# Linear attention and a cosine feed-forward layer on one core: the key maxima as two float32r parts, the projection loaded by ScalarE, another order table

## The chip, the cores and the metric

The kernel runs on one core of one Trainium2 chip. A core has five engines with queues of their own: TensorE (PE in the profile; its weight loads are shown as PEld), VectorE (DVE), ScalarE (ACT), GpSimd (POOL) and SyncE (SP), which here only starts transfers. Each engine takes its instructions strictly in order, and waits at an instruction until the semaphores that it needs have been raised. The metric is the device time of one execution in microseconds (us). Of the kernel before there are three times, 1094.05, 1092.6 and 1094.47 us, with a median of 1094.05 us.

## The reference

For 8 batches and 8 heads, with 576 positions and 64 channels a head:

```python
def phi(x):
    proj = np.einsum('bhsd,df->bhsf', x, w_phi)                 # 64 -> 128 features
    proj = proj - np.max(np.abs(proj), axis=-1, keepdims=True)
    return np.concatenate([np.exp(proj), np.exp(-proj)], axis=-1)
q_p, k_p = phi(q), phi(k)
kv  = np.einsum('bhsf,bhsd->bhfd', k_p, v);  z = np.sum(k_p, axis=2)
num = np.einsum('bhsf,bhfd->bhsd', q_p, kv)
den = np.einsum('bhsf,bhf->bhs', q_p, z)[..., None] + 1e-06
x   = (num / den)                       # then 4608 tokens x 512 channels
h   = x @ w_in                          # 512 -> 2048
out = (h * np.cos(h)) @ w_out           # 2048 -> 512
```

Each row of a projection has its largest absolute value taken off before the two exponentials. That subtraction, for the keys, is what the change touches.

## The kernel before

**Two stages, interleaved.** The attention is cut into 32 units `u` of two heads each (`attention(u)`, L427). The feed-forward layer is cut into 15 visits `v` of a block of 512 tokens and a list of 128-wide slices of the hidden layer (`visit(v)`, L741). The weights of the layer are split once into two float32r parts, a high and a low one (`convert(ft)`, L353), so that three fast float32r products stand for one float32 product: twelve matmuls of 128x128 by 128x512 per first product (L798), and four times three per second product (L832 to L834). The attention matmuls are plain float32, which TensorE runs as two passes: one matmul in the code is two records in the trace.

**The keys of a unit.** `k_mm` (L493) and its tail (`k_end`, L568) project the keys into three PSUM banks, two of 128x512 and one of 128x128. VectorE takes the row maxima (`k_max`, L580): a 128x4 tile for each of the two large banks, 128x1 for the tail. In units 0 to 7 (`K_SUMS = range(8)`) TensorE then adds the negated maxima to the bank itself (`k_sub`, L590): the weights are `minus`, a 128x128 matrix with -1 on its diagonal, and the moving operand is the tile of maxima, each value repeated 128 times by a broadcast view. ScalarE reads the bank and writes both exponentials (`exp_k`, L598). In units 8 to 31 VectorE subtracts instead (L585). The exponentials go into the sums `kv` and `z` (`kv_mm`, L642 and L648), which ScalarE copies out of PSUM.

**The queries.** `q_mm` (L455) projects them, ScalarE copies the result (L462), VectorE reduces it across partitions (L466, L474, L476), spreads the maxima (L480), GpSimd subtracts (`q_sub`, L484), and ScalarE takes the exponentials (L603). `z_mm` (L681) and `n_mm` (L691) form denominators and numerators, and VectorE divides.

**Order.** All work is built as `Step` objects, each with its engine and a function that issues its instructions. A table of step numbers, `ORDER` (L86), gives one order for all of them, and each engine's queue is that order cut down to its own steps. Nothing is reordered later. `plan()` (L240) goes over the table and gives each PSUM tile one of eight banks: before the change it keeps a clock for each engine, adds up the steps' written costs, and takes the bank that comes free first by that clock. The costs and the names `port` and `table` serve only that choice.

**Start.** SP loads `w_phi` into both halves of `wphi` (L309), then the queries and keys of unit 0 and of unit 1, then the first weights. GpSimd writes `halfpi`, `minus` and the constant columns of the value tiles. On GpSimd's queue lie the subtractions for the queries and the last three steps of the first four weight slices (L387, L54 and L393).

Of the kernel before, what the change touches and what calls it, by code (L numbers as in the profile page):

```python
# [17 lines left out]
P = 128  # L18
# [7 lines left out]
def phi_attention_then_cos_ffn(ctx: ExitStack, tc: tile.TileContext, qT, kT, vS, vT, w_phi, w_in, w_out, out):  # L26
# [41 lines left out]
    class Step:  # L68
# [15 lines left out]
    SWITCH = dict(e=1.3, s=1.3, full=0.21, left=0.145, quarter=0.12, upper=0.2)  # L84
    SHAPE = dict(mm1="full", mm2="full", one="full", k_mm="upper", k_end="full", t_mm="upper", t_end="full", s_mm="full", k_sub="full", kv_mm="left", n_mm="left", z_mm="quarter", q_mm="upper")
    ORDER = [  # L86
# [151 lines left out]
    LATENCY = dict(PE=0.35, ACT=0.25, DVE=0.2, POOL=0.25, SP=2.2)  # L238

    def plan():  # L240
        free = dict.fromkeys(LATENCY, 0.0)
        free["port"] = 0.0
        table = {}
        last = {}
# [702 lines left out]
```

## Time and profile before

| | |
|---|---|
| median of the three times | 1094.05 us |
| time of the profiled execution | 1094.05 us |
| its span in the trace | 1092.3 us |
| outside the span (difference of the two) | 1.75 us |
| TensorE busy | 1075.4 us, 98% of the span |
| VectorE busy | 725.2 us, 66% |
| ScalarE busy | 717.2 us, 66% |
| GpSimd busy | 127.3 us, 12% |
| TensorE clock granted | 1.00 |

"Busy" is the time in which at least one instruction of the engine was running. Matmuls overlap, so the duration of a matmul in the trace is longer than the time that it keeps the next one away: the distance from start to start is the cost in a row of matmuls. A line such as `PE bank L590 <- DVE mk_u__850 L580: 1.3, 1, 1.3` in the view of waits says that TensorE, at line 590, stood idle for 1.3 us in total, once, 1.3 us at longest, until VectorE's line 580 had written `mk`.

### The profile page before, as it was taken

To read this page: it belongs to the slowest core of one execution; us is meant where nothing else is said; L and a number is where in the kernel's file an instruction comes from. 1 tells how busy PE (TensorE), PEld (TensorE's weight loads), DVE (VectorE), ACT (ScalarE), POOL (GpSimd) and SP (SyncE) were. 2 spreads that over 40 slices of the span, in tenths; PEclk is the share of its full clock that TensorE was granted. 3 is DMA by queue.
4 is the path that set the end of the run, shared out by engine and by line. 5 is a ranking of instruction groups with operands and counts; after the bars stand their busy time and mean duration, and the time that the engine had idled before them with its cause. 6 is when DMAs were issued, how large, how long until landed. Compare 5 with 4: busy or idle time off the path is not lost.

```text
span 1092.3 us, 19509 instructions
## 1 busy us (share of the span) xinstructions
PE 1075.4 (98%) x7664; PEld 827.7 (76%) x7664; DVE 725.2 (66%) x1298; ACT 717.2 (66%) x1386; POOL 127.3 (12%) x91
## 2 busy tenths in 40 slices
PE   7999999999999999999999999999999999999998
PEld 4656666778888887788677787787777778888886
DVE  5899999989889868555577366773665354343432
ACT  5888889977666587657567666857667654443533
POOL 2654221000000011101031011110111000000000
PEclk9999999999999999999999999999999999999999
DMA  6564664356667355555241651345211620630441
GB/s 193 150 192 121 193 193 142 97 167 208 224 203 242 109 196 159 195 180 222 55 149 69 205 185 46 106 176 192 93 61 61 250 99 2 222 125 20 146 191 48
DMA packets 92603, 160.71 MB, mean 147 GB/s; under 512 B 43744, under 2 KB 52064, under 8 KB 84320
## 3 DMA queue, kind: packets, MB, share of 16 engines
q1 hardware_dynamic: 92512, 159.48, 43.9%
q8 instruction: 60, 0.98, 0.4%
q14 instruction: 31, 0.25, 0.1%
HBM read 117.51 MB, written 41.94 MB: 146 GB/s over the span
## 4 chain that ended last, share of the span: by engine, by line
PE 86%; DVE 6%; issue 0%; DMA 0%; ACT 0%; DVEq 0%
PE bank L798 35%; PE bank L832 12%; PE bank L833 12%; PE bank L834 12%; PE bank L691 4%; PE bank L642 4%; PE bank L681 2%; PE bank L455 2%; PE bank L493 2%; PE bank L648 1%; PE bank L568 0%; DVE g_c__1102 L809 0%; DMA out<-o_last 0%; DVE m_u__975 L466 0%; DVE g_c__1972 L809 0%
## 5 line engine op out<-in xcount | busy, mean ns | idle before, releaser
L813 ACT ACT_TABLE_LOAD x22 | 28.2, 1283 | 0.4
L484 POOL TENSOR_TENSOR pq_u__3673<-pq_u__3673,bq_u__4170 128x576 f32<-128x576 f32 x2 | 3.6, 1796 | 186.1 <-DVE bq_u__4170 L480 186.1
L872 DVE TENSOR_TENSOR o<-bank,o 128x512 f32<-128x512 f32 x24 | 16.2, 679 | 0.7 <-DMA o<-sums 0.5
L881 DVE COPY o<-bank 128x512 f32<-128x512 f32 x16 | 10.8, 677 | 5.9 <-PE bank L834 4.7
L603 ACT ACT_TABLE_LOAD x11 | 14.1, 1283 | 0.2
L879 ACT ACTIVATE o<-bank 128x512 f32<-128x512 f32 x16 | 9.5, 593 | 5.5 <-PE bank L834 5.5
L598 ACT ACT_TABLE_LOAD x10 | 12.8, 1283 | 0.2
L798 PE MATMUL bank<-xh_c__7472,w 128*128 128x512 f32 x32 | 12.8, 400 | 0.0
L798 PE MATMUL bank<-xh_c__6688,w 128*128 128x512 f32 x32 | 12.8, 399 | 0.0
L798 PE MATMUL bank<-xh_c__5272,w 128*128 128x512 f32 x32 | 12.8, 399 | 0.0
L798 PE MATMUL bank<-xh_c__4458,w 128*128 128x512 f32 x32 | 12.7, 396 | 0.0
L798 PE MATMUL bank<-xh_c__7041,w 128*128 128x512 f32 x32 | 12.5, 390 | 0.0
L798 PE MATMUL bank<-xh_c__5868,w 128*128 128x512 f32 x32 | 12.5, 390 | 0.0
L798 PE MATMUL bank<-xh_c__8219,w 128*128 128x512 f32 x32 | 12.5, 390 | 0.0
L798 PE MATMUL bank<-xh_c__5790,w 128*128 128x512 f32 x32 | 12.5, 390 | 0.0
L798 PE MATMUL bank<-xh_c__7889,w 128*128 128x512 f32 x32 | 12.5, 390 | 0.0
L798 PE MATMUL bank<-xh_c__6645,w 128*128 128x512 f32 x32 | 12.5, 390 | 0.0
L798 PE MATMUL bank<-xh_c__5941,w 128*128 128x512 f32 x32 | 12.5, 390 | 0.0
L798 PE MATMUL bank<-xh_c__4514,w 128*128 128x512 f32 x32 | 12.5, 390 | 0.0
L798 PE MATMUL bank<-xh_c__4696,w 128*128 128x512 f32 x32 | 12.5, 390 | 0.0
L798 PE MATMUL bank<-xh_c__7074,w 128*128 128x512 f32 x32 | 12.5, 390 | 0.0
L798 PE MATMUL bank<-xh_c__8223,w 128*128 128x512 f32 x32 | 12.5, 390 | 0.0
(3837 smaller groups left out, 4061.7 us busy)
## 6 DMA issues: line engine op xcount, KB each, us to landing
w<-w_parts SPq DMA_DIRECT2D x48, 1024.0 KB, 5.0
w_parts<-w SPq DMA_DIRECT2D x16, 1024.0 KB, 5.5
vmain<-vS SPq DMA_DIRECT2D x32, 256.0 KB, 4.7
out<-o SPq DMA_DIRECT2D x32, 256.0 KB, 3.0
sums<-o SPq DMA_DIRECT2D x24, 256.0 KB, 3.3
o<-sums SPq DMA_DIRECT2D x24, 256.0 KB, 3.2
vtail<-vT SPq DMA_DIRECT2D x64, 16.0 KB, 3.7
out<-o_last SPq DMA_DIRECT2D x4, 256.0 KB, 2.0
```

The costliest lines, as they stand in the source:

```text
L455: PE.matmul(out=ps[j], lhsT=wphi[r, :], rhs=d["qr"][r, hf * HALF:(hf + 1) * HALF], start=True, stop=True)
L493: PE.matmul(out=ps[j][:, P * s:P * s + P], lhsT=x[r, P * s:P * s + P], rhs=wphi[r, :], start=(s == 0), stop=w, skip_group_check=True)
L603: ACT.activation(out=e[:, s, :], in_=d["pq"][:, j * S:(j + 1) * S], func=AF.Exp, scale=1.0 - 2.0 * s)
L642: PE.matmul(out=acc[c:c + 64, n, i, :], lhsT=e[:, s, P * n + c:P * n + c + 64], rhs=vmain[u % 2][:, s, i, :], start=(s == 0 and i == 0 and ...
L681: PE.matmul(out=ps[32 * g:32 * g + 32], lhsT=d["z"][:, 2 * n + j, :], rhs=d["eq", j][:, n, hf * HALF:(hf + 1) * HALF], start=(n == 0), sto ...
L691: PE.matmul(out=d["nps", hf][64 * j:64 * j + 64], lhsT=d["kv"][:, 2 * n + j, :], rhs=d["eq", j][:, n, cut[hf]], start=(n == 0 and hf == 0) ...
L798: PE.matmul(out=h, lhsT=a[:, cs], rhs=d[b, kt], start=(k == 0), stop=(k == 3 * KT - 1))
L813: ACT.activation(out=m["g"], in_=m["g"], func=AF.Sin, bias=halfpi, scale=1.0)
L832: PE.matmul(out=a, lhsT=gh[:, t], rhs=w[:, 0], start=first, stop=False)
L833: PE.matmul(out=a, lhsT=gh[:, t], rhs=w[:, 1], start=False, stop=False)
L834: PE.matmul(out=a, lhsT=gl[:, t], rhs=w[:, 0], start=False, stop=last)
L872: DVE.tensor_tensor(out=o, in0=bank(acc[tb]), in1=o, op=ALU.add)
```

## The change

1. **The maxima in two parts.** A new step `k_parts` on GpSimd stands between `k_max` and `k_sub` in units 0 to 7, three to a unit, 24 in all. It writes a float32r copy of the maxima (`hi_of`, one `tensor_scalar`) and the float32r remainder (`lo_of`, one `tensor_tensor`), each 128x4 or 128x1. `k_sub` issues two float32r matmuls in place of one in float32. `minus` becomes float32r, made from `minus_f` by one more GpSimd instruction at the start.
2. **The projection's load** is issued by ScalarE's queue instead of SP's.
3. **Seven extra matmuls** (`WARM = 7`) of a zeroed 128x128 float32 tile by itself go to bank 7 ahead of the planned steps. VectorE zeroes the tile. Their result is not used.
4. **Another order table**, with the 24 new steps. On every engine but GpSimd it holds the same steps as before. Counted in the two tables: matmul steps that differ in tile shape from the one before them on TensorE are 180 before and 173 after, and changes of ScalarE's function table are 44 before and 46 after.
5. **`plan()`** gives a new PSUM tile the bank whose last user stands earliest in the table, and no longer uses costs. The costs written at the steps are changed too, and decide nothing any more.

```diff
-    ORDER = [
-        0, 41, 2, 5, 3, 6, 7, 4, 8, 10, 11, 43, 46, 16, 57, 9, 12, 1192, 18, 20, 13, 44, 45, 48, 61, 19, 17, 58, 21,
...
+        place = {steps[x]: i for i, x in enumerate(ORDER)}
+        owner = [None] * len(banks)
+
+        def last(b):
+            return -1 if b is None else max(place[v] for v in b.users)
...
+                    b.slot = min(range(len(banks)), key=lambda i: last(owner[i]))
...
-        SP.dma_start(out=wphi[64 * j:64 * j + 64, :], in_=w_phi)
+        ACT.dma_start(out=wphi[64 * j:64 * j + 64, :], in_=w_phi)
...
-    minus = const.tile([P, P], F32, name="minus")
-    POOL.memset(minus, -1.0)
-    POOL.affine_select(out=minus, in_=minus, pattern=[[-1, P]], compare_op=ALU.is_equal, fill=0.0, base=0,
+    warm = const.tile([P, P], F32, name="warm")
+    DVE.memset(warm, 0.0)
+
+    minus_f = const.tile([P, P], F32, name="minus_f")
+    POOL.memset(minus_f, -1.0)
+    POOL.affine_select(out=minus_f, in_=minus_f, pattern=[[-1, P]], compare_op=ALU.is_equal, fill=0.0, base=0,
                        channel_multiplier=1)
+    minus = const.tile([P, P], F32R, name="minus")
+    hi_of(POOL, minus, minus_f)
...
+    WARM = 7
...
+        def k_parts(i):
+            tag = "pk" if i < 2 else "pk_t"
+            m = d["mk", i]
+            p = d["mp", i] = new(tag, [P, 2, NSLOT if i < 2 else 1], F32R, f"mp_u{u}_", "mp" + tag)
+            hi_of(POOL, p[:, 0], m)
+            lo_of(POOL, p[:, 1], m, p[:, 0])
+
         def k_sub(i):
...
-            PE.matmul(out=pv, lhsT=minus, rhs=d["mk", i].unsqueeze(2).broadcast_to([P, n, P]), start=False, stop=True,
-                      skip_group_check=True)
+            for r in range(2):
+                PE.matmul(out=pv, lhsT=minus, rhs=d["mp", i][:, r].unsqueeze(2).broadcast_to([P, n, P]), start=False,
+                          stop=(r == 1), skip_group_check=True)
...
             if u in K_SUMS:
-                kms[i] = Step("PE", 0.86 if i < 2 else 0.22, lambda i=i: k_sub(i), [kms[i]], use=[kb[i], pks[i]], kind="a.k_sub")
+                kms[i] = Step("POOL", 0.35, lambda i=i: k_parts(i), [kms[i]], use=[pks[i]], port=True, kind="a.k_parts")
+                kms[i] = Step("PE", 0.46 if i < 2 else 0.14, lambda i=i: k_sub(i), [kms[i]], use=[kb[i], pks[i]], kind="a.k_sub")
...
+        for _ in range(WARM):
+            PE.matmul(out=banks[7][:, 0:P], lhsT=warm, rhs=warm, start=True, stop=True, skip_group_check=True)
         for x in plan():
             x.fn()
```

The heads of the queues that the new table gives, in step names (unit in brackets): TensorE `k_end(0)`, two `q_mm(0)`, `k_sub(0)` of the tail, `q_mm(1)`, `k_mm(0)`, `q_mm(1)`, `k_end(1)`, `k_mm(1)`, three `k_sub`, then `kv_mm(0)`; before, four `q_mm`, `k_mm(0)`, `k_mm(1)`, `k_sub(0)`, two `k_end`, four `k_sub`, then `kv_mm(0)`. ScalarE: four `q_copy(0)`, `exp_k(0)` of the tail, four `q_copy(1)`, the first `w.scale` (L371 and L372), the two large `exp_k(0)`. SP: loads of unit 0 and unit 1, first weights, values of unit 0, as before. GpSimd: three `k_parts(0)` and one `k_parts(1)`, then the first `q_sub(0)`, with the other `k_parts` between subtractions and weight steps from there on.

More of the change, by code (lines that the diff above doesn't have):

```diff
@@ L356, in convert @@
         slot = w_slot[ft] = Buf("w")
-        name, eng, cost = ("POOL", POOL, 2.4) if ft in W_POOL else ("DVE", DVE, 1.22)
+        name, eng, cost = ("POOL", POOL, 2.4) if ft in W_POOL else ("DVE", DVE, 1.135)
         def load():
@@ L609, in attention @@
             d["kb", i] = kb[i]
-        main = Step("PE", 0.88, lambda: k_mm(0), [ld], take=kb[:2] + pks[:2], use=[b["kr"]], kind=phase + "k_mm")
-        tail = Step("PE", 0.22, lambda: k_mm(1), [ld], take=[kb[2], pks[2]], use=[b["kr"]], kind=phase + "k_end")
+        main = Step("PE", 0.89, lambda: k_mm(0), [ld], take=kb[:2] + pks[:2], use=[b["kr"]], kind=phase + "k_mm")
+        tail = Step("PE", 0.14, lambda: k_mm(1), [ld], take=[kb[2], pks[2]], use=[b["kr"]], kind=phase + "k_end")
         for i in range(3):
-            cost = (1.3 if i < 2 else 0.55) if u not in K_SUMS else 0.67 if i < 2 else 0.28
+            cost = (1.32 if i < 2 else 0.51) if u not in K_SUMS else 0.6 if i < 2 else 0.21
             kms.append(Step("DVE", cost, lambda i=i: k_max(i), [tail if i == 2 else main], use=[kb[i], pks[i]],
@@ L621, in attention @@
             e = Buf("ek" if i < 2 else "ek_t")
-            eks.append(Step("ACT", 1.06 if i < 2 else 0.42, lambda i=i: exp_k(i), [kms[i]] + gate, take=[e], use=[pks[i]] + ([kb[i]] if u in K_SUMS else []),
+            eks.append(Step("ACT", 1.045 if i < 2 else 0.4, lambda i=i: exp_k(i), [kms[i]] + gate, take=[e], use=[pks[i]] + ([kb[i]] if u in K_SUMS else []),
                             table="e", kind=phase + "exp_k"))
@@ L667, in attention @@
                         kind=phase + "kv_mm")
-        ko = Step("ACT", 0.6, kv_out, [last], use=[acc, b["kv"]], kind=phase + "kv_out")
+        ko = Step("ACT", 0.45, kv_out, [last], use=[acc, b["kv"]], kind=phase + "kv_out")
         N0 = CT
```

70 lines of the change are left out of this document (20 added, 50 removed), and 300 rows, old and new, of the table ORDER.

## The prediction

> **What bounds the kernel now.** I read the page's first part, then busy time by stretches, then TensorE's waits. The stretches have these columns: from and to, length, then busy time and number of instructions of PE, PEld, DVE, ACT and POOL, the granted clock, the DMA share and GB/s.
>
> ```profile
> PE 1075.4 (98%) x7664; PEld 827.7 (76%) x7664; DVE 725.2 (66%) x1298; ACT 717.2 (66%) x1386; POOL 127.3 (12%) x91
> ```
>
> ```profile
> 0.00:5.00 5.00, 0.00 (x0) 0.00 (x0) 0.00 (x0) 1.28 (x1) 1.42 (x15) 1.00 0.36 102
> 5.00:30.00 25.00, 21.98 (x213) 14.79 (x214) 18.49 (x38) 16.49 (x40) 9.30 (x6) 1.00 0.62 192
> 30.00:100.00 70.00, 67.95 (x798) 43.46 (x797) 65.11 (x122) 59.41 (x130) 39.28 (x21) 1.00 0.48 146
> 100.00:200.00 100.00, 97.66 (x1089) 65.38 (x1089) 94.56 (x201) 87.18 (x193) 24.21 (x17) 1.00 0.56 173
> 200.00:1000.00 800.00, 799.97 (x5181) 631.61 (x5181) 514.03 (x891) 516.63 (x962) 53.13 (x34) 1.00 0.44 147
> 1000.00:1088.00 88.00, 87.86 (x388) 72.44 (x386) 32.32 (x49) 36.21 (x63) 0.00 (x0) 1.00 0.30 108
> 1088.00:1092.30 4.30, 0.00 (x0) 0.00 (x0) 0.69 (x1) 0.00 (x0) 0.00 (x0) 0.89 0.65 245
> ```
>
> TensorE is the bound. From 200 to 1000 us it is idle for 0.03 us, so each microsecond of its work that goes away, and each wait that goes away ahead of 200 us, comes off the end. All its idle time is 16.9 us (1092.3 less 1075.4): 5.27 us before the first matmul, some 4.4 us after the last one, where the last tile is copied and stored, and 7.1 us of waits in between, nearly all of them ahead of 200 us. There VectorE is almost as full: 65.11 of 70 us and 94.56 of 100 us. That is the stage in which the change lies.
>
> ```profile
> PE bank L455 <- DMA qr_u__117<-qT: 5.3, 1, 5.3
> PE bank L590 <- DVE mk_u__293 L580: 1.6, 1, 1.6
> PE bank L590 <- DVE mk_u__850 L580: 1.3, 1, 1.3
> PE bank L455 <- DMA qr_u__121<-qT: 1.1, 1, 1.1
> PE bank L798 <- DVE pk_u__1058 L585: 0.8, 1, 0.8
> ```
>
> The first wait is the start. Of the others only two are waits of `k_sub` for its maxima, so 22 of the 24 subtractions now find them ready.
>
> **The subtraction in two parts.** Four neighbours in the timeline give the float32 price by start distances, and one row of the chain gives the float32r price (start, length, engine, line):
>
> ```profile
> 72.57 0.38 PE L590 MATMUL bank<-mk_u__940,minus 128*128 128x128 f32 x2
> 72.79 1.02 PE L590 MATMUL bank<-mk_u__936,minus 128*128 128x512 f32 x2
> 73.65 1.02 PE L590 MATMUL bank<-mk_u__930,minus 128*128 128x512 f32 x2
> 74.60 1.24 PE L455 MATMUL bank<-qr_u__789,wphi 64*128 64x288 f32 x8
> ```
>
> ```profile
> 1038.90 8.16 PE bank L798 x36
> ```
>
> A large float32 `k_sub` keeps TensorE for 73.65 - 72.79 = 0.86 us, a tail for 72.79 - 72.57 = 0.22 us. Float32r with 512 columns costs 8.16/36 = 0.227 us, so two parts cost 0.45 us, and 16 large ones save 16 x 0.41 = 6.5 us. No row shows float32r with 128 columns. Its bounds are a quarter of 0.227 us a part (0.11 us for two) and no gain at all (0.22 us). I take 0.16 us, halfway, so 8 tails save 0.5 us, with 0 to 0.9 us as ends. That the moving operand is a broadcast view is no new cost, since the float32 form has the same view. **Sum: -7.0 us.**
>
> **The order's own work on TensorE.** The tables hold the same steps, with 7 fewer changes of tile shape. The price of one:
>
> ```profile
> 82.06 0.50 PE L798 MATMUL bank<-xh_c__439,w 128*128 128x512 f32 x1
> 82.40 0.40 PE L798 MATMUL bank<-xh_c__660,w 128*128 128x512 f32 x1
> ```
>
> After a change the next matmul starts 82.40 - 82.06 = 0.34 us later, against 0.227 us in a row: 0.11 us each. **-0.8 us**, with 0 and twice that as ends, as the shapes differ.
>
> **The start.** Rows of the timeline, and landing times of the transfers (last column, us from issue):
>
> ```profile
> 0.81 1.21 SPq L309 DMA_DIRECT2D wphi<-w_phi  x2
> 2.07 0.58 SPq L437 DMA_DIRECT2D qr_u__117<-qT  x1
> 2.69 0.43 SPq L438 DMA_DIRECT2D kr_u__118<-kT  x1
> 5.27 2.29 PE L455 MATMUL bank<-qr_u__117,wphi 64*128 64x288 f32 x8 [5.27 <-DMA qr_u__117<-qT]
> 6.60 0.41 ACT L462 ACTIVATE pq_u__130<-bank 128x288 f32<-128x288 f32 x1 [4.51 <-PE bank L455]
> 8.67 2.29 PE L455 MATMUL bank<-qr_u__121,wphi 64*128 64x288 f32 x8 [1.10 <-DMA qr_u__121<-qT]
> 10.75 1.92 PE L493 MATMUL bank<-wphi,kr_u__118 64*128 64x128 f32 x16
> ```
>
> ```profile
> 59.94 1.24 PE L455 MATMUL bank<-qr_u__610,wphi 64*128 64x288 f32 x8
> 67.93 1.06 PE L493 MATMUL bank<-wphi,kr_u__798 64*128 64x128 f32 x16
> ```
>
> ```profile
> kr_u__118<-kT SPq DMA_DIRECT2D x1, 320.0 KB, 3.4
> wphi<-w_phi SPq DMA_DIRECT2D x2, 32.0 KB, 2.1
> ```
>
> With `wphi` on ScalarE's queue SP issues everything 1.26 us earlier (2.07 - 0.81). ScalarE does nothing then but load a table, so two issues of 0.6 us there cost nothing while its first real work starts at 6.6 us. TensorE's first step is now `k_end(0)`, which needs the keys, the second transfer: issued at 1.4 us, landing 3.4 us later, 4.8 us. That is **-0.5 us**. The ends are 0, if `wphi` is what arrives last, and -1.26 us.
>
> Early matmuls run at half pace: `q_mm` of a unit takes 2.29 us twice, and 1.24 us at 60 us; `k_mm(0)` takes 1.92 us against 1.06 us. That is 2 x 1.05 + 0.86 = 3.0 us. The granted clock in the rows reads 1.00 throughout, so it does not show this. The seven extra matmuls fall into idle time ahead of the data: each is two passes of 128 columns at half pace, so about twice the tail's 0.22 us, seven make 3.1 us, from about 1.1 to 4.2 us. A gap of 0.6 us to the data follows. In the rows the pace doubled only after some 3.5 us without a gap (from 8.67 us; the 2.3 us ahead of the gap there were not enough). I take two thirds of the 3.0 us: **-2.0 us**, with 0 and -3.0 us as ends. The Trainium skill, "TensorE: Matmul & The Clock Gate", section "What's actually happening", says that the clock follows a free-running window of about 3.4 us, so the warm-up is a time and not a count of matmuls; the case's trace agrees with that length, and by the rule the seven alone fall short of a full window, so that the gain would be anything between the two ends, run by run.
>
> **Waits that move.** ScalarE's new queue puts the first weight scaling ahead of the two large `exp_k(0)`:
>
> ```profile
> 12.41 1.14 ACT L371 ACTIVATE w_t_f__193<-w_raw_f__166 128x1024 f32<-128x1024 f32 x1 [0.99 <-DMA w_raw_f__166<-w_out]
> 14.75 1.08 ACT L598 ACTIVATE ek_u__198<-bank 128x512 f32<-128x512 f32 x2 [0.20 <-PE bank L590]
> 18.04 1.15 PE L642 MATMUL bank<-vmain,ek_u__198 128*64 128x65 f32 x32
> 24.44 0.49 PE L590 MATMUL bank<-mk_u__293,minus 128*128 128x128 f32 x2 [1.65 <-DVE mk_u__293 L580]
> 25.96 0.27 PE L691 MATMUL bank<-eq_u__268,kv_u__274 128*64 128x64 f32 x1
> ```
>
> The scaling starts when its weights land, at 12.41 - 1.26 = 11.15 us; its two instructions take 2.2 us, the exponentials 1.1 us, and 0.2 us go to the handover: the first `kv_mm` can start at 14.6 us, against 18.04 us. From there to the first `n_mm` TensorE took 7.9 us, 1.65 us of it waiting at a `k_sub(2)` that now stands behind that `n_mm`: with the 0.5 us that two cheaper `k_sub` save on this way, 14.6 + 6.3 - 0.5 = 20.4 us, against 25.96 us, 5.5 us earlier. All six `k_sub` ahead of it account for 1.8 us, start and pace for 2.5 us, and the other 1.2 us are waits saved. I count 0.8 of them, as other steps change places too: **-0.8 us**, with 0 and the 1.65 us of that wait as ends.
>
> Against it stands the detour through GpSimd. No row shows a small arithmetic instruction there. Bounds are
>
> ```profile
> 0.98 0.11 POOL L322 MEMSET vmain<- 128x8 f32 x1
> 1.45 0.29 POOL L315 TENSOR_SCALAR_AFFINE_SELECT minus<-minus 128x128 f32<-128x128 f32 x1
> ```
>
> 0.11 us for a write of 128x8 and 0.29 us for a pass over 128x128: two instructions take 0.22 to 0.58 us, and with one more handover each maximum arrives about 0.6 us later. Behind a waiting `k_sub` stands all of TensorE's queue, and `exp_k` with its `kv_mm` is late next. Where other matmuls stand between `k_max` and `k_sub`, as for 22 of 24 now, they hide it; without that cover it is 24 x 0.6 = 14 us. I take 1.5 us, the two that already wait and a fraction of the rest: **+1.5 us**, ends 0 and, for all of them exposed by half, 7 us. The extra instruction on `minus` and the zeroing of `warm` lie in the first 5 us, ahead of any use. Two more table loads cost ScalarE 2.6 us, in stretches where it has 13 us to spare in 100. The bank choice changes no instruction.
>
> **Sum:** -7.0 - 0.8 - 0.5 - 2.0 - 0.8 + 1.5 = -9.6 us. The profiled execution is its span 1092.3 us and 1.75 us around it, 1094.05 us, which is the median of the three. Forecast: **1084.5 us**.
>
> **Rivals.** *The waits shrink further* (12%). All 7.1 us of waits are there to be removed, and the keys no longer hold TensorE. If the new table removes 4 us more than I count and the detour stays hidden, the time is 1084.5 - 1.5 - 4 = 1079 us. Against it: VectorE has little idle time to give.
>
> *VectorE becomes the bound* (18%). In the stretch from 30 to 200 us VectorE idles for 10.3 us (4.89 + 5.44). Its work does not shrink, so TensorE can come forward only by VectorE's earlier start, 1.3 us, and by what VectorE's idle time can give. With half of that the gain ends at 1.3 + 5.2 = 6.5 us: 1087.5 us. Speaks for it: three of the four waits shown behind the start are for VectorE. Against it: the table can put more second-layer matmuls, which ask less of VectorE, among the units.
>
> *Two parts cost as much as one float32 product* (6%). If a broadcast float32r operand ran at float32's pace the 7.0 us would be missing: 1091.5 us. Line 798's 0.227 us speaks against it.
>
> *GpSimd and VectorE get in each other's way* (9%), the slower side:
>
> ```profile
> L476 DVE TENSOR_TENSOR m_u__287<-m_u__286 x4: 185/186/2285, 21.1 to 23.9; 32x36 f32<-32x36 f32 x4
> 21.00 2.35 POOL L387 TENSOR_TENSOR w_t_f__195<-w_t_f__195,w_t_f__193 128x1024 f32<-128x1024 f32 x1 [2.79 <-ACT eq_u__271 L603]
> ```
>
> A 0.186 us instruction of VectorE took 2.285 us from 21.1 us on, just while GpSimd's 2.35 us multiplication ran. Each `k_parts` is a new reader there. If its 0.4 us stops VectorE each time, that is 24 x 0.4 = 9.6 us on the fuller engine, with VectorE as the bound as above: 1094.05 - 6.5 + 9.6 = 1097 us. It decides from about 6.5 us of added stops, and below that it only eats the gain. Against it: VectorE's maxima are read from PSUM, and its long stops come from the 2.4 us instructions, which stay as they are. The Trainium skill, "SBUF — State Buffer", section "Who interferes with whom", holds that the pair of ports is locked for a whole instruction and the other engine fully blocks; the 2.285 us agree.
>
> **How the numbers follow.** 55% for the forecast; its own range from the bounds is 1080 to 1088 us. The rivals have 12, 18, 6 and 9%. The range of 1079 to 1091.5 us leaves out the slower rival and a little of the fastest. A measurement of this kernel tells about 0.2%, 2.2 us, from no change. Faster by that holds for the forecast, the first two rivals and a part of the third, 0.87; 0.05 stays within it; 0.08 is slower.
>
> **What would show it.** Line `k_sub` as float32r with starts 0.23 us apart; TensorE's busy time lower by 9 to 11 us; matmuls ahead of 5 us, and `q_mm(0)` near 1.3 us; first `kv_mm` near 14.6 us and first `n_mm` near 20.5 us; waits of `k_sub` on GpSimd of 1 to 2 us in total; idle TensorE from 200 us on still near zero. Wrong would be: waits ahead of 200 us above 12 us, VectorE idle there as long as now, many small VectorE instructions of over 0.4 us, or new waits for weights behind 200 us.

## The result, and the profile after

The changed kernel takes 1108.09 us (median of four executions, 1106.01 to 1109.66), the kernel before 1094.07 us beside it: a ratio of 1.0129, with a 95% interval of 1.0110 to 1.0149. It is 14.0 us slower, where 9.6 us faster was forecast, and outside the range. The profiled execution took 1109.66 us, 1107.7 us of them its span.

In the changed kernel all lines after the start have other numbers: `k_end` is L548, `k_max` L560, VectorE's subtraction L565, `k_sub` L578, `k_mm` L473, `q_mm` L435, `z_mm` L670, `n_mm` L680, `invert` L686. The two instructions of `k_parts` are recorded under their helpers, L51 and L54. First the busy line of the page and the busy time by stretches, with the columns explained in the prediction.

```profile
PE 1077.8 (97%) x7678; PEld 835.6 (75%) x7678; DVE 735.2 (66%) x1299; ACT 718.5 (65%) x1388; POOL 140.2 (13%) x140
```

```profile
30.00:70.00 40.00, 39.98 (x550) 26.21 (x549) 37.39 (x75) 37.93 (x92) 29.45 (x41) 1.00 0.58 177
70.00:120.00 50.00, 41.34 (x386) 28.52 (x386) 48.40 (x87) 37.16 (x74) 21.10 (x18) 0.97 0.43 145
120.00:200.00 80.00, 77.38 (x898) 53.27 (x893) 73.05 (x155) 69.19 (x156) 18.11 (x12) 0.98 0.47 144
200.00:400.00 200.00, 200.00 (x1062) 162.45 (x1062) 172.20 (x252) 138.40 (x235) 6.43 (x4) 1.00 0.56 189
400.00:600.00 200.00, 190.55 (x1455) 145.64 (x1454) 122.30 (x228) 124.22 (x246) 19.12 (x12) 0.97 0.41 138
```

TensorE is idle for 1107.7 - 1077.8 = 29.9 us, 13.0 us more than before. Of the 29.9 us, 9.45 us lie between 400 and 600 us, where TensorE had been busy throughout, and 8.66 us between 70 and 120 us, where VectorE is now at 48.40 of 50 us. The busy time did not fall but rose by 2.4 us, although the subtraction became cheaper; 3.36 us of it are the seven extra matmuls. Three stretches show a clock below 1.00. In the first two (1 - 0.97) x 50 + (1 - 0.98) x 80 = 3 us of full pace are missing, as far as two decimals tell; for the third see the narrower rows below. The longest waits of TensorE name the places:

```profile
PE bank L680 <- DVE dn_u__4563 L686: 5.4, 1, 5.4
PE bank L680 <- DVE dn_u__4825 L686: 3.4, 1, 3.4
PE bank L578 <- POOL mp_u__1174 L51: 1.9, 1, 1.9
PE bank L548 <- DVE pk_u__1298 L565: 1.8, 1, 1.8
PE bank L473 <- DVE pk_u__2314 L565: 1.5, 1, 1.5
PE bank L680 <- DVE dn_u__1578 L686: 1.4, 1, 1.4
```

The two largest are `n_mm` behind `invert`, a pair of steps that the prediction never mentions. The timeline at the first of them (start, length, engine, line), the stretches ahead of it and behind it, and the stretch behind the second:

```profile
410.38 0.44 DVE L686 TRANSPOSE_TENSOR_REDUCE dn_u__4563<-bank 128x9 f32<-128x288 f32 x1
410.87 0.37 PE L680 MATMUL bank<-eq_u__4328,kv_u__4422 128*64 128x64 f32 x1 [5.42 <-DVE dn_u__4563 L686]
411.35 1.06 PE L680 MATMUL bank<-eq_u__4328,kv_u__4422 128*64 128x512 f32 x1
```

```profile
405.00:411.00 6.00, 0.58 (x6) 0.13 (x4) 5.86 (x11) 3.80 (x6) 0.00 (x0) 0.80 0.08 31
411.00:420.00 9.00, 9.00 (x99) 5.94 (x100) 2.91 (x8) 2.33 (x8) 0.00 (x0) 0.76 0.10 31
445.00:450.00 5.00, 5.00 (x22) 2.43 (x23) 2.87 (x7) 0.00 (x0) 0.00 (x0) 0.66 0.83 270
```

TensorE stands still for 5.42 us while VectorE works without a break (5.86 of 6 us) through its queue towards a reduction of 0.44 us. Then it runs with the clock at 0.76, and behind the second wait at 0.66: 9 x 0.24 + 5 x 0.34 = 3.9 us of full pace are missing behind the two. The code says why it waits:

```python
d["nps", 0], d["nps", 1] = bank(nps)[:, 0:N0], bank(zps)[:, HALF:HALF + S - N0]   # z_mm
PE.matmul(out=d["nps", hf][64 * j:64 * j + 64], ...)                              # n_mm
DVE.tensor_reduce(out=dn, in_=d["zps"].rearrange("p (j t) -> p j t", t=32), ...)  # invert
```

`n_mm` writes its last 64 columns into the bank in which `invert` reads the denominators. They are other columns, but it is one tile, and so the two steps are ordered by their places in the table. Whichever stands second waits for the other. In the table before, `n_mm` of units 16 and 31 stood ahead of `invert`, and `n_mm` of unit 15 stood 74 places behind it, time enough for VectorE. In the new table `invert` stands ahead in all three units, 1 to 4 places before its `n_mm`. In unit 7 it stood 8 places ahead and now stands 7 ahead, with other work of VectorE before it; that is the wait of 1.4 us. The place alone does not make a wait: in the table before, `invert` stood ahead by 5 to 8 places in units 10, 22 and 27 as well, and that trace has no wait for `dn`. It takes a VectorE that comes late.

### The profile page after: what moved, and what is told of

It is laid out like the page before. It is cut to its first block, busy times and chain, and to the rows that moved or that the text cites. A ratio compares the mean times of both kernels' runs of the same rounds, so it can differ in the third digit from the quotient of the medians.

```text
span 1107.7 us, 19590 instructions
## 1 busy us (share of the span) xinstructions
PE 1077.8 (97%) x7678; PEld 835.6 (75%) x7678; DVE 735.2 (66%) x1299; ACT 718.5 (65%) x1388; POOL 140.2 (13%) x140
## 4 chain that ended last, share of the span: by engine, by line
PE 83%; DVE 6%; ACT 2%; DMA 1%; issue 1%; SPq 0%; DVEq 0%
PE bank L787 33%; PE bank L821 11%; PE bank L822 11%; PE bank L823 11%; PE bank L680 5%; PE bank L631 4%; PE bank L670 2%; PE bank L435 2%; PE bank L473 2%; PE bank L637 1%; PE bank L548 0%; DMA qr_u__1767<-qT 0%; DVE m_u__1213 L456 0%; DMA o<-sums 0%; DVE g_c__1244 L798 0%
## 5 line engine op out<-in xcount | busy, mean ns | idle before, releaser
L787 PE MATMUL bank<-xh_c__6814,w 128*128 128x512 f32 x32 | 13.1, 410 | 0.0
L787 PE MATMUL bank<-xh_c__4554,w 128*128 128x512 f32 x32 | 12.8, 401 | 0.0
L787 PE MATMUL bank<-xh_c__5459,w 128*128 128x512 f32 x32 | 12.8, 400 | 0.0
L787 PE MATMUL bank<-xh_c__8108,w 128*128 128x512 f32 x32 | 12.7, 396 | 0.0
L787 PE MATMUL bank<-xh_c__6987,w 128*128 128x512 f32 x32 | 12.5, 392 | 0.0
L787 PE MATMUL bank<-xh_c__6816,w 128*128 128x512 f32 x32 | 12.5, 392 | 0.0
L787 PE MATMUL bank<-xh_c__4756,w 128*128 128x512 f32 x32 | 12.5, 392 | 0.0
L787 PE MATMUL bank<-xh_c__7212,w 128*128 128x512 f32 x32 | 12.5, 391 | 0.0
L787 PE MATMUL bank<-xh_c__4731,w 128*128 128x512 f32 x32 | 12.5, 391 | 0.0
L787 PE MATMUL bank<-xh_c__4810,w 128*128 128x512 f32 x32 | 12.5, 391 | 0.0
L787 PE MATMUL bank<-xh_c__5372,w 128*128 128x512 f32 x32 | 12.5, 390 | 0.0
L787 PE MATMUL bank<-xh_c__8235,w 128*128 128x512 f32 x32 | 12.5, 390 | 0.0
L787 PE MATMUL bank<-xh_c__6016,w 128*128 128x512 f32 x32 | 12.5, 390 | 0.0
L787 PE MATMUL bank<-xh_c__8243,w 128*128 128x512 f32 x32 | 12.5, 390 | 0.0
L787 PE MATMUL bank<-xh_c__7897,w 128*128 128x512 f32 x32 | 12.5, 390 | 0.0
L787 PE MATMUL bank<-xh_c__5919,w 128*128 128x512 f32 x32 | 12.5, 390 | 0.0
L787 PE MATMUL bank<-xh_c__9384,w 128*128 128x512 f32 x32 | 12.5, 390 | 0.0
```

Source lines behind the costliest of these rows:

```text
L787: PE.matmul(out=h, lhsT=a[:, cs], rhs=d[b, kt], start=(k == 0), stop=(k == 3 * KT - 1))
```

## The experiments

All of them in one table. The kernel before ran beside each group, and runs of different groups are compared by the difference from it.

| kernel | median, us | before beside it, us | difference, us | ratio, 95% interval |
|---|---|---|---|---|
| changed kernel | 1108.09 | 1094.07 | +14.0 | 1.0110 to 1.0149 |
| changed, `invert` behind `n_mm` | 1092.19 | 1094.03 | -1.8 | 0.9974 to 0.9993 |
| changed, old bank choice | 1107.71 | 1093.75 | +14.0 | 1.0109 to 1.0139 |
| before, parts alone | 1102.81 | 1094.03 | +8.8 | 1.0071 to 1.0101 |
| before, parts, four GpSimd steps moved | 1098.59 | 1092.91 | +5.7 | 1.0026 to 1.0056 |
| before, new bank choice alone | 1104.29 | 1093.87 | +10.4 | 1.0077 to 1.0109 |
| changed, old table | 1112.36 | 1094.03 | +18.3 | 1.0154 to 1.0186 |
| changed, no parts | 1109.38 | 1094.03 | +15.4 | 1.0128 to 1.0162 |
| `invert` moved, weight steps in pieces | **1088.28** | 1092.91 | **-4.6** | 0.9946 to 0.9971 |
| the same, no parts | 1090.72 | 1093.87 | -3.2 | 0.9959 to 0.9981 |
| the same, old bank choice | 1089.06 | 1093.75 | -4.7 | 0.9955 to 0.9978 |
| the same, ten extra matmuls | 1088.99 | 1093.87 | -4.9 | 0.9945 to 0.9971 |
| `invert` moved, ten extra matmuls | 1092.42 | 1092.91 | -0.5 | 0.9987 to 1.0005 |
| before, weight steps in pieces | 1092.56 | 1092.91 | -0.4 | 0.9989 to 1.0007 |
| before, start alone | 1092.54 | 1093.87 | -1.3 | 0.9977 to 0.9994 |

### Where the 14 us are: the four late steps, and the banks

**First run: `invert` behind `n_mm`.** The changed kernel with six entries of the table moved; each engine's queue keeps its order, so that only the direction changes in which each pair waits. Entries 345, 633, 669 and 1209 are `invert` of units 7, 15, 16 and 31, and 348, 636, 672 and 1212 their `n_mm`; 1210 and 1211 are the two steps behind the last `invert`.

```diff
-  ... 344, 1377, 1400, 345, 1397, 390, 375, 391, 1384, 392, 348, 393 ...
+  ... 344, 1377, 1400, 1397, 390, 375, 391, 1384, 392, 348, 345, 393 ...
-  ... 633, 636 ...     669, 1335, 748, 702, 672 ...     1209, 2556, 1210, 1211, 1212 ...
+  ... 636, 633 ...     1335, 748, 702, 672, 669 ...     2556, 1212, 1209, 1210, 1211 ...
```

> The changed kernel with four steps moved by a few places in the table: invert of units 7, 15, 16 and 31 stands right behind its unit's n_mm and no longer ahead of it. Every engine's queue is the same; only the direction of the conflict on the shared bank changes. Theory A: the two waits of n_mm for VectorE (5.4 and 3.4 us at 405 and 441 us) and the slow matmuls behind them go, 1092 to 1097 us. If the late VectorE work only makes another wait in its place: 1104 to 1108 us.

It took 1092.19 us, 15.9 us less than the changed kernel. Its busy line, one of its stretches and its longest waits:

```profile
PE 1069.9 (98%) x7678; PEld 830.9 (76%) x7678; DVE 734.6 (67%) x1299; ACT 718.3 (66%) x1388; POOL 140.2 (13%) x140
```

```profile
70.00:120.00 50.00, 41.30 (x388) 27.52 (x384) 48.40 (x89) 37.70 (x74) 20.21 (x18) 1.00 0.45 149
```

```profile
PE bank L548 <- DVE pk_u__1298 L565: 2.9, 1, 2.9
PE bank L578 <- POOL mp_u__1174 L51: 1.8, 1, 1.8
```

No wait for `dn` is left. The span fell by 17.6 us: TensorE's idle time by 29.9 - 20.2 = 9.7 us, and its busy time by 7.9 us with the same matmuls. Of the 7.9 us, 3.9 us are the half pace behind the two longest waits. Another 3.3 us are half pace from 76 to 82 us and from 180 to 184 us (6 x 0.28 + 4 x 0.41), behind waits of 1.85 and 1.53 us. This kernel has the same two waits, and in its profiled execution the clock stayed at 1.00 behind them, so these 3.3 us can't be put down to the edit. So the two longest waits, 8.8 us of standing still, took some 3.9 us of slow matmuls with them. This one matter, four steps on the wrong side of their partner, is the whole of the loss of 14 us; without it the changed kernel is within 0.2% of the one before.

**Second run: the old bank choice in the changed kernel.**

```diff
-                    b.slot = min(range(len(banks)), key=lambda i: last(owner[i]))
+                    at, b.slot = empty(x.eng)
...
```

> The changed kernel with one edit: PSUM banks are chosen as before, by a clock that adds up the steps' written costs. Theory (the bank choice by position is a second cause with the new table too, as it costs the old table 10 us): the two waits behind invert stay, the small bank waits go, and 1101 to 1105 us. Rival (with the new table the bank choice costs nothing): 1106.5 to 1109.5 us.

1107.71 us, with the waits of 5.4 and 3.4 us unchanged. In the new table the bank choice costs nothing, as the rival said. The same diff applied to the best version below:

> The changed table with the late steps moved and GpSimd's weight steps in four pieces (1088.3 us), with banks chosen by the clock of written costs. Theory (the waits of k_end, k_mm and z_mm on VectorE's subtractions, 4.3 us in the profile, are for a bank that another choice would not have given): those waits gone, 1083 to 1086 us. Rival (they are VectorE's lateness, whatever the bank): 1087.5 to 1089.5 us, with waits of other matmuls on VectorE of the same sum.

It is 4.7 us below the kernel before, where that version is 4.6 us below. The waits of 1.7 and 1.5 us for VectorE are still in place, so they are VectorE's lateness and not the bank's.

### The parts of the change in the old table

**The two parts alone.** The kernel before, with `k_parts`, the float32r `minus` and two matmuls in `k_sub`; each `k_parts` stands in the table right behind its `k_max`.

```diff
+                kms[i] = Step("POOL", 0.35, lambda i=i: k_parts(i), [kms[i]], use=[pks[i]], port=True, kind="a.k_parts")
-                kms[i] = Step("PE", 0.86 if i < 2 else 0.22, lambda i=i: k_sub(i), ...
+                kms[i] = Step("PE", 0.46 if i < 2 else 0.14, lambda i=i: k_sub(i), ...
```

> The kernel before, with the maxima in two float32r parts on GpSimd as the only change: each k_parts stands in the old order table right behind its k_max. Theory A (the new order table is what costs, the parts are a gain): TensorE's subtraction falls from 18.75 us to about 11 us, little of it is given back in waits, 1086 to 1089 us. Theory B (the detour through GpSimd and its stops of VectorE are what costs): waits of k_sub and long VectorE instructions eat the 7 us and more, 1094 us or above.

1102.81 us: 8.8 us slower. The longest wait in its view of waits, and GpSimd's rows of the timeline ahead of the maxima that it waits for:

```profile
PE bank L602 <- POOL mp_u__922 L51: 5.3, 1, 5.3
```

```profile
68.74 2.35 POOL L54 TENSOR_TENSOR w_t_f__878<-w_t_f__878,w 128x1024 f32<-128x1024 f32 x1 [2.25 <-DVE mk_u__925 L584]
71.05 1.40 POOL L488 TENSOR_TENSOR pq_u__740<-pq_u__740,bq_u__875 128x576 f32<-128x576 f32 x1
72.41 0.19 POOL L51 TENSOR_SCALAR mp_u__922<-mk_u__920 128x1 fp32r<-128x1 f32 x1
```

The detour's own work is 0.19 us. Ahead of it in GpSimd's queue stand a weight step of 2.35 us and a subtraction for the queries of 1.40 us, and TensorE's whole queue stands behind the `k_sub`. From 30 to 70 us its clock is 0.91, from 70 to 120 us 0.93. The edit also changed the two written costs, on which that bank choice rests, so a part of the 8.8 us may be a moved bank; the waits for `mp`, 10.7 us in the five longest rows, are enough to carry it.

**The same with four GpSimd steps moved behind the parts** (two additions and one remainder of weight slices 0 to 2, one subtraction of unit 4).

```diff
-  ... 1222 ... 157 ...      1230 ... 242 ...      1237, 191 ... 245 ...
+  ... 157, 1222 ...         242, 1230 ...         245, 1237, 191 ...
```

> The parts alone in the old order (1102.8 us), with four steps of GpSimd moved: the last step of weight slices 0 and 1, the second step of slice 2 and one query subtraction of unit 4 stand behind the k_parts that they stood ahead of. Every other queue is the same. Theory D (the detour costs by what stands ahead of it in GpSimd's queue, and the slow matmuls follow from TensorE's gaps): the waits of 5.3, 2.7 and 1.4 us go and most of the half-paced matmuls with them, 1088 to 1092 us. If the detour itself costs: 1100 us or more.

1098.59 us, 5.7 us slower than before, and in neither of the two ranges. The wait of 5.3 us is gone and 3.1 us with it, but other parts now wait (2.8 and 1.4 us), and the clock from 30 to 70 us is still 0.91. Place in GpSimd's queue is a part of the cost, shown; that it is all of it was not shown.

**The bank choice alone.** The kernel before with the new `plan()`.

```diff
-                    at, b.slot = empty(x.eng)
+                    b.slot = min(range(len(banks)), key=lambda i: last(owner[i]))
...
```

> The kernel before with one edit: a new PSUM tile gets the bank whose last user stands earliest in the order table, as in the changed kernel; order table, k_sub, start stay as before. Theory (the bank choice by position is what separates the two kernels with the old table, 1112.4 and 1102.8 us): new waits of matmuls for a bank that ScalarE or VectorE has not yet read, of 3 us and more each, and 1100 to 1105 us. Rival (the bank choice costs nothing by itself, and the difference came from the earlier start meeting the old table): 1092 to 1096 us and no wait of that kind above 1 us.

1104.29 us. So this edit, which changes no instruction, costs the old table 10.4 us. Two of its waits, and the stretch behind the first:

```profile
PE bank L771 <- DVE pk_u__1058 L558: 3.6, 1, 3.6
PE bank L615 <- ACT hs_c__2038 L778: 3.3, 1, 3.3
```

```profile
80.00:90.00 10.00, 6.35 (x29) 4.77 (x28) 9.27 (x15) 4.03 (x10) 6.58 (x4) 0.67 0.09 31
```

The first is the wait of the first product for VectorE's `pk_u__1058` that the prediction quoted at 0.8 us. Idle time rose by 7.1 us to 24.0 us and busy time by 4.7 us: again two long waits, and half pace behind them.

**All of it but the order.** The changed kernel with the old table (each `k_parts` behind its `k_max`). Only the table differs: the old order of steps, under the new numbers.

```diff
     ORDER = [
-        0, 44, 1216, 17, 2, 5, 3, 6, 7, 4, 24, 25, 26, 46, 16, 49, 61, 8, 10, 11, 9, 12, 18, 21, 68, 13, 29, 19, 22,
+        0, 44, 2, 5, 3, 6, 7, 4, 8, 10, 11, 46, 49, 16, 60, 9, 12, 1216, 18, 19, 21, 22, 13, 47, 48, 51, 65, 66, 20,
...
```

> The changed kernel with the old order table (k_parts right behind k_max): parts, ScalarE's load of the projection, seven extra matmuls and the bank choice by table position all stay. Theory A: within 2 us of the parts alone in the old order, so 1085 to 1090 us. Theory B: 1094 us or above. If the parts alone are near 1087 us and this is above 1092 us, the bank choice or the start costs.

1112.36 us, 18.3 us slower. It shows both kinds of wait, 5.3 us for `mp` and 4.3 and 3.3 us for banks. Parts (+8.8), banks (+10.4) and start (-1.3, below, there with ten extra matmuls) add up to 17.9 us. So parts and bank choice need another table, and the one that came with them does away with what they cost, but for its four late steps.

### What the two parts are worth

**The changed kernel without them**, with one float32 matmul on the maxima as before.

```diff
-            for r in range(2):
-                PE.matmul(out=pv, lhsT=minus, rhs=d["mp", i][:, r].unsqueeze(2).broadcast_to([P, n, P]), start=False,
-                          stop=(r == 1), skip_group_check=True)
+            PE.matmul(out=pv, lhsT=minus, rhs=d["mk", i].unsqueeze(2).broadcast_to([P, n, P]), start=False, stop=True,
+                      skip_group_check=True)
```

> The changed kernel without the parts: k_parts is taken out of the new table, and k_sub is one float32 matmul again. Theory A: the order's loss without the parts' gain, 1108 plus 5 to 8 us, 1112 to 1117 us. Theory B: the loss goes with the detour, 1098 us or below.

1109.38 us, in neither of the two ranges, with the same waits of 5.4 and 3.4 us. The parts are worth 1.3 us there, less than the spread. The same diff applied to the best version:

> The same kernel as the one with four pieces (1088.3 us), without k_parts: k_sub is one float32 matmul on the maxima, as before. It tells what the two parts are worth once the late steps are out of the way. Theory by the prediction's sum (TensorE bounds, so its 7 us of saved work reach the end): 1094 to 1096 us. Rival (all subtractions lie ahead of some 150 us, where VectorE bounds, so the saved TensorE time is idle time there): 1088.5 to 1090.5 us, with TensorE busier by 6 to 7 us ahead of 200 us and its waits shorter by as much.

It is 3.2 us below the kernel before, the best version 4.6 us: the parts are worth some 1.5 us by the medians, though the two intervals in the table overlap. That is close to the rival's range. What the rival named as the sign did not come: ahead of 200 us TensorE is busy for 191.26 us in place of 189.98, 1.3 us more and not 6 to 7. Where the rest goes is seen in the first `n_mm` of units 0, 3, 11 and 12, and in the stretch ahead of the last. First the kernel with parts, then the one without:

```profile
24.44 0.27 PE L685 MATMUL bank<-eq_u__244,kv_u__313 128*64 128x64 f32 x1
...
58.09 0.27 PE L685 MATMUL bank<-eq_u__830,kv_u__745 128*64 128x64 f32 x1
...
164.24 0.27 PE L685 MATMUL bank<-eq_u__2188,kv_u__2265 128*64 128x64 f32 x1
...
176.91 0.27 PE L685 MATMUL bank<-eq_u__2342,kv_u__2413 128*64 128x64 f32 x1
```

```profile
172.00:176.00 4.00, 3.83 (x17) 2.24 (x18) 3.85 (x9) 3.05 (x9) 0.71 (x1) 0.57 0.22 66
```

```profile
22.71 0.27 PE L673 MATMUL bank<-eq_u__220,kv_u__287 128*64 128x64 f32 x1
...
59.56 0.27 PE L673 MATMUL bank<-eq_u__768,kv_u__683 128*64 128x64 f32 x1
...
165.61 0.27 PE L673 MATMUL bank<-eq_u__2090,kv_u__2167 128*64 128x64 f32 x1
...
176.76 0.27 PE L673 MATMUL bank<-eq_u__2244,kv_u__2315 128*64 128x64 f32 x1
```

```profile
172.00:176.00 4.00, 3.32 (x31) 2.37 (x35) 3.97 (x8) 3.46 (x13) 2.06 (x2) 1.00 0.02 3
```

At unit 0 the kernel with parts is 1.73 us behind; its profiled execution had `k_mm(0)` at 1.92 us, the other at 1.06 us. Between units 0 and 3 the parts gain 3.2 us (33.65 against 36.85 us), about what the twelve subtractions in between save. From there to unit 11 the lead grows no more, 1.47 and then 1.37 us, although six subtractions are still to come. In that stretch VectorE is full in both kernels, with 48.4 of 50 us between 70 and 120 us. The lead is not given back there either. It goes in one step, between units 11 and 12: both kernels wait for 1.52 us for the same step of VectorE, and the one with parts falls to half pace right after it (clock 0.57) and the other does not (1.00). That the lead grows no more fits a stretch that VectorE limits, which no run tests apart; the rest of the loss is half pace in the one execution that was profiled. What other executions keep of the lead stays open.

### GpSimd's long instructions and VectorE

In the kernel with `invert` moved TensorE is still busy for only 41.30 of 50 us between 70 and 120 us. VectorE's four small maxima of one unit, 0.74 us by the price of 0.186 us each, stand for 5.09 us there. GpSimd's row and VectorE's; another weight step of 2.38 us follows on GpSimd:

```profile
81.80 2.39 POOL L367 TENSOR_TENSOR w_t_f__1115<-w_t_f__1115,w_t_f__1113 128x1024 f32<-128x1024 f32 x1 [4.22 <-DVE w_t_f__1113 L360]
81.91 5.09 DVE L456 TENSOR_TENSOR m_u__1213<-m_u__1212 32x36 f32<-32x36 f32 x4
```

**Four pieces.** That kernel, with GpSimd's three weight steps (multiplication, remainder, addition) of slices 0 to 3 each issued as four instructions of 256 columns.

```diff
-            eng.tensor_tensor(out=d["t2"], in0=d["t2"], in1=d["t0"].bitcast(F32), op=ALU.mult)
+            for c in cols:
+                eng.tensor_tensor(out=d["t2"][:, c], in0=d["t2"][:, c], in1=d["t0"].bitcast(F32)[:, c], op=ALU.mult)
...
```

> The changed kernel with the four steps moved (1092.2 us) and GpSimd's twelve weight instructions of 1024 columns (slices 0 to 3) each cut into four of 256. Theory C (VectorE sets the stretch from 70 to 120 us because whole 2.4 us instructions of GpSimd stop its small ones): the stops of 2.3 us shrink to about 0.6 us, 3 to 6 us of TensorE's waits between 70 and 120 us go, 1086 to 1089 us. If VectorE's own work is the bound there and the stops only fill its idle time: 1091 to 1093 us. The pieces cost GpSimd about 0.1 us each, 3.6 us in all.

**1088.28 us**, 4.6 us below the kernel before. It beats both kernels. The same place there:

```profile
81.65 2.79 POOL L370 TENSOR_TENSOR w_t_f__1142<-w_t_f__1142,w_t_f__1140 128x256 f32<-128x256 f32 x4 [4.21 <-DVE w_t_f__1140 L362]
81.76 2.74 DVE L461 TENSOR_TENSOR m_u__1240<-m_u__1239 32x36 f32<-32x36 f32 x4
```

VectorE gets in between the pieces: 2.74 us in place of 5.09 us. GpSimd takes 0.4 us longer for this step, and its busy time rises by 6.1 us in all (146.3 against 140.2 us). TensorE's busy time in the stretch rises from 41.30 to 45.88 us, and 2.8 us come off the end (4.6 less 1.8). The place is right: the first `n_mm` of unit 5 starts at 85.41 us in place of 85.56, that of unit 6 at 101.71 us in place of 105.77. The Trainium skill, "SBUF — State Buffer", section "Who interferes with whom", says that a VectorE instruction with two inputs in SBUF contends with a GpSimd instruction that reads there, which is this pair, and that tensor_reduce does not; the 5.09 us agree with the first, and no run here tests the second.

**The same pieces in the kernel before**, with the same diff.

> The kernel before, with GpSimd's weight instructions cut into four pieces as the only change. Theory C: VectorE's three stops of 2.3 us go, but TensorE waits for VectorE only some 3 us there, 1091 to 1094 us. No more than 1 us either way says that the stops cost the kernel before nothing.

1092.56 us, no difference that can be told. There the stops cost nothing. They became a cost only with the new table, in which TensorE waits for VectorE behind them.

### The start

In the changed kernel the start went like this:

```profile
1.11 3.36 PE L892 MATMUL bank<-warm 128*128 128x128 f32 x14 [1.11 <-DVE warm L288]
5.72 0.77 PE L548 MATMUL bank<-wphi,kr_u__129 128*128 128x128 f32 x2 [1.26 <-DMA wphi<-w_phi]
6.42 2.29 PE L435 MATMUL bank<-qr_u__128,wphi 64*128 64x288 f32 x8
...
10.38 1.92 PE L473 MATMUL bank<-wphi,kr_u__129 64*128 64x128 f32 x16
```

The extra matmuls end at 4.47 us, the projection arrives 1.26 us later, and `q_mm(0)` and `k_mm(0)` keep their half pace of 2.29 and 1.92 us in this execution. The projection lands 3.8 us after its issue on ScalarE's queue, beside the queries and keys; on SP's queue, ahead of them, it took 2.1 us. So the first matmul on data starts at 5.72 us, 0.45 us later than before. The first `n_mm` starts at 25.10 us, 0.9 us earlier than before.

**Ten extra matmuls**, in the kernel with `invert` moved, and then in the one with pieces too.

```diff
-    WARM = 7
+    WARM = 10
```

> The changed kernel with the four steps moved and ten extra matmuls in place of seven, so that they end at about 5.9 us, where the projection lands, and leave no gap. If the pace of the first matmuls follows a stretch of work without gaps: q_mm of unit 0 takes about 1.3 us in place of 2.29 us, 1089 to 1091 us. If three more leave the pace as it is: 1092 to 1093 us.

> The changed table with the late steps moved and GpSimd's weight steps in four pieces (1088.3 us), and ten extra matmuls in place of seven. Theory (with VectorE relieved, the 1.5 to 2 us that a faster pace saves ahead of 12 us now reach the end): 1085.5 to 1087 us. Rival (VectorE still bounds from 70 to 200 us and gives an earlier start back): 1087.5 to 1089 us, although k_mm(0) takes 1.05 us in place of 1.92 us.

Below the kernel before by 0.5 us (1.8 with seven), and by 4.9 us (4.6 with seven). In the profile of the first the pace is what it was with seven: `q_mm(0)` 2.29 us and `k_mm(0)` 1.05 us in both. That run does not test an earlier change of pace. In the second the pace did double earlier, with `q_mm(0)` at 1.24 us and this `k_mm(0)`:

```profile
8.33 1.06 PE L478 MATMUL bank<-wphi,kr_u__132 64*128 64x128 f32 x16
```

It did not last: from 22 to 26 us, behind a wait of 1.23 us, the clock is 0.59 and 0.56. In unit 3 this execution still leads by 1.0 us (57.09 against 58.09 us), from unit 5 on by 0.36 us (85.05 against 85.41 us), and no gain is left that the medians could tell.

**The start alone in the kernel before**: the projection loaded by ScalarE, and ten extra matmuls.

```diff
-        SP.dma_start(out=wphi[64 * j:64 * j + 64, :], in_=w_phi)
+        ACT.dma_start(out=wphi[64 * j:64 * j + 64, :], in_=w_phi)
...
+    warm = const.tile([P, P], F32, name="warm")
+    DVE.memset(warm, 0.0)
...
+        for _ in range(10):
+            PE.matmul(out=banks[7][:, 0:P], lhsT=warm, rhs=warm, start=True, stop=True, skip_group_check=True)
```

> The kernel before with the start of the change alone: the projection loaded by ScalarE, and ten extra matmuls of a zeroed tile; order table, k_sub and bank choice as before. Theory by the prediction's sum (an earlier start and a faster pace reach the end): q_mm(0) starts 0.5 us or more earlier, k_mm(0) near 1.05 us, and 1089.5 to 1091.5 us. Rival (VectorE, 94% busy from 100 to 200 us, gives it back): the same start, but 1092.3 to 1094.5 us.

1092.54 us: 1.3 us faster. Its first `n_mm` starts at 23.41 us, 2.55 us earlier than before. The median lies in the rival's range, but for another reason than the rival's: in the profiled execution VectorE gives nothing back. At unit 11 the lead is still 2.70 us (166.74 against 169.44 us), behind a stretch in which VectorE is busy for 47.97 of 50 us, and the whole span is 2.6 us shorter. In the median a half of it arrives. How much reaches the end from one execution to the next stays open.

## Why the prediction was wrong

**The step that failed** is "**Waits that move**", with the sentence it rests on, that from 200 to 1000 us TensorE is idle for 0.03 us and so only savings matter there. I sized the new order by its first 26 us and took the rest to keep the old kernel's absence of waits. That absence was a property of the old table. Two pairs of `invert` and `n_mm` changed sides in the new one and a third lost its distance; where the prediction put nothing, TensorE waited behind `invert` for 5.42, 3.40 and 0.6 us in these and for 1.4 us in unit 7, with slow matmuls behind the two long waits. Putting `invert` second in all four took 15.9 us off. The table itself was at hand: for each pair of steps on two engines that share a tile, which one stands first, and how much work its engine has ahead of it. The list of what would prove the forecast wrong did ask for new waits behind 200 us, but looked for weights.

**The price of a wait** was also wrong in kind. The prediction counted a wait as its idle time. Here 8.8 us of waiting took some 3.9 us of slow matmuls with it.

Term by term:

- *The subtraction, -7.0 us.* Right in mechanism, a little large, and little of it shows at the end. These rows of the changed kernel give the new prices by their starts:

```profile
14.98 0.33 PE L578 MATMUL bank<-mp_u__198,minus 128*128 128x128 f32 x2
15.15 0.65 PE L578 MATMUL bank<-mp_u__195,minus 128*128 128x512 f32 x2
...
19.50 0.70 PE L578 MATMUL bank<-mp_u__225,minus 128*128 128x512 f32 x2
20.04 0.60 PE L578 MATMUL bank<-mp_u__228,minus 128*128 128x512 f32 x2
20.56 0.76 PE L435 MATMUL bank<-qr_u__299,wphi 64*128 64x288 f32 x4
```

  A large one costs 0.52 to 0.54 us, not 0.45, and a tail 0.17 us, as taken. That is 16 x 0.33 + 8 x 0.05 = 5.7 us of TensorE's time. But the prediction let "each microsecond of its work" ahead of 200 us come off the end, right beside its own rows with VectorE at 94%. Of the 5.7 us, 1.3 and 1.5 us arrived by the medians, neither clear of the spread. The rival *VectorE becomes the bound* may have a part of this right, the six last subtractions, about 1.4 us. Half pace behind a wait that the sum left out cost as much in the profiled execution.
- *Shape changes, -0.8 us.* Not measured alone. TensorE's busy time with `invert` moved, less the 3.36 us of extra matmuls, is 1066.5 us, 8.9 us below before and near the 9 to 11 us forecast: the sum of TensorE's own work was about right.
- *Start, -0.5 and -2.0 us.* The projection arrived last, as the end of 0 had it, and later than the prediction allowed: the first matmul on data came 0.45 us later than before, not 0.5 us earlier. Seven matmuls did not change the pace in the profiled execution of the changed kernel, and did in others, and even ten brought no gain that the medians could tell.
- *Waits at the head of the queues, -0.8 us.* The first `kv_mm` came at 16.63 us, not 14.6, and the first `n_mm` at 25.10 us, not 20.4.
- *Detour through GpSimd, +1.5 us.* One wait of 1.9 us: right for this table. In the old one it cost 8.8 us and the saving with it, by the run with the parts alone, and the 14 us named for a lost cover were the honest warning.
- *Banks, 0 us.* Right here, but for the wrong reason. "Changes no instruction" is no argument: it moved waits worth 10.4 us in the old table.
- *GpSimd against VectorE.* A cost of 2.8 us, shown by the four pieces. The rival had the right engines and the wrong culprit: the long weight steps stopped VectorE, not `k_parts`. The prediction had these steps in view, but took their price to stay as it was.

## What to carry to other kernels

When an order is replaced, go through every pair of steps on two engines that touch the same tile, in the whole table and not at its head, and see which side each stands on and how much work the other engine has ahead of it: four such pairs were worth 15.9 us here, more than the whole forecast gain. Price a long wait of TensorE above its length. Before a difference of 1 to 3 us between two profiles gets a cause, lay the starts of the same step in both side by side and look at the clock where they part: here a short wait with half pace behind it, met in one execution and not in the other, looked like an engine that gives time back. A long instruction of GpSimd may cost nothing until a better order has TensorE wait for VectorE behind it; cutting it in four is then cheap.

## What the runs showed of the hardware that was not expected

- After waits of 5.42 and 3.40 us in the changed kernel and of 3.6 us in the kernel with the bank choice alone matmuls ran at half pace for some microseconds, and the clock column shows it (0.76 from 411 to 420 us, 0.66 from 445 to 450 us, 0.67 from 80 to 90 us). The change of pace need not come at once. Behind the wait of 3.40 us `n_mm` begins at the full pace and is slowed 1.1 us later:

```profile
444.99 0.27 PE L680 MATMUL bank<-eq_u__4445,kv_u__4612 128*64 128x64 f32 x1 [3.40 <-DVE dn_u__4825 L686]
445.27 0.59 PE L680 MATMUL bank<-eq_u__4445,kv_u__4612 128*64 128x512 f32 x1
446.14 1.06 PE L680 MATMUL bank<-eq_u__4445,kv_u__4612 128*64 128x512 f32 x1
```

- A short wait can have half pace behind it as well, and the same wait in another execution has none. First the changed kernel, then the one with `invert` moved:

```profile
76.85 0.78 PE L578 MATMUL bank<-mp_u__1174,minus 128*128 128x512 f32 x2 [1.85 <-POOL mp_u__1174 L51]
```

```profile
76.00:82.00 6.00, 5.15 (x15) 3.62 (x16) 5.84 (x12) 5.08 (x11) 2.14 (x6) 0.72 0.01 2
```

```profile
76.00 0.77 PE L578 MATMUL bank<-mp_u__1174,minus 128*128 128x512 f32 x2 [1.84 <-POOL mp_u__1174 L51]
```

```profile
76.00:82.00 6.00, 5.58 (x23) 4.32 (x24) 5.78 (x12) 5.15 (x11) 1.76 (x3) 1.00 0.00 0
```

  So it is with a longer one: behind the wait of 2.9 us the clock is 1.00 from 91 to 96 us in the kernel with `invert` moved, and 0.66 in the same kernel with ten extra matmuls. The length of the wait alone does not decide, and what does stays open. The Trainium skill, "TensorE: Matmul & The Clock Gate", section "What's actually happening", puts the way back to half pace behind an idle window of about 3.4 us. These traces differ: waits of 1.23, 1.53 and 1.85 us were enough in some executions, in the kernel with the bank choice alone even two of 0.37 and 0.15 us (0.79 from 142 to 150 us), and the measurement decides.
- With seven extra matmuls ahead of the start `k_mm(0)` took 1.92 us in the changed kernel and in the one with pieces, 1.05 us in the one with `invert` moved and 1.06 us in the one with pieces and without parts. At this length the gain is a matter of the execution.
- Two float32r matmuls with 128 columns took 0.17 us, and with 512 columns 0.53 us, a little over twice the 0.227 us of a long row of them.
- GpSimd's small instruction on 128x4 or 128x1 took 0.18 to 0.20 us in 41 of 48 cases in the changed kernel; the dearer part of its price was its place in the queue. The other seven took 0.24 to 1.19 us. The longest began at 17.34 us, 0.1 us behind a VectorE instruction of 1.23 us, and both ended at 18.5 us.
